# One planned order for all of attention, the channel MLPs and the second mixture's weights

## The chip, the cores and the metric

The kernel runs on one core of one Trainium2 chip. The metric is device time in microseconds (us) of one execution; lower is better. Engine names are those of the profile: PE (TensorE matmul), DVE (VectorE), ACT (ScalarE), POOL (GpSimd) and SP (SyncE, whose queue issues nearly all DMAs).

## What is computed

Four batches, 768 positions, 8 heads of 48, model width 384. First a linear attention with a complex decay per channel, then a mixture with a low-rank token mix and a channel MLP, then a second mixture with trigonometric gates:

```python
for t in range(S):                                  # attention, 768 steps
    S_re, S_im = ar * S_re - ai * S_im + kv, ar * S_im + ai * S_re
    y[:, :, t] = np.einsum('bhd,bhde->bhe', q[:, :, t], S_re)
...
h = xt @ U @ V                                      # first mixture
u = x + h.transpose(0, 2, 1)
x = u + np.maximum(u @ w_ch1, 0.0) @ w_ch2
...
theta = x @ w_theta                                 # second mixture
y = w_tok_r @ (x * cos(theta)) + w_tok_i @ (x * sin(theta))
u = x + y
out = u + np.maximum(u @ w_ch, 0.0)
```

The weights arrive as 64-bit floats and are unpacked on the chip into a high and a low 32-bit part, so most products are three matmuls (high by high, high by low, low by high).

## The kernel before, in words

**Attention.** The 768 positions are cut into 6 chunks of 128, and chunks go in pairs: 3 pairs for each batch, 12 in all. `ew` computes a pair's decay products on ACT and DVE in the store `er` (for pair 1 alone in the store made of `wa` and `wb`). For a pair this is some 20 operations over 128x768 elements, two kinds of scans (L358 and L385), and table loads on ACT. At its end four products a pair (L337, `tt2`) write what `gather` then moves by DMA into the tile `QK`. `pe_steps` then does a chunk on PE: scores (L453), their copy on ACT (L459) and mask on POOL (L463), transposes of k (L469), state update (L492), output (L521), a transpose back (L535), and `gx` (L546), which collects the low-rank product of a batch. When all six chunks of a batch are in, `g_steps` adds the low-rank mix to the batch's tokens (`hx`, L576 on PE, L581 on DVE). Only then can that batch's MLP start.

**MLP.** `mlp_steps` works on a batch as 3 groups of 256 tokens, and a group as 6 pairs of an F unit (18 matmuls, L711) and a C unit (12 matmuls, L736). So there are 72 of each. After an F unit, ACT writes `rh` (L716) and DVE `rl` (L721), which the next C unit reads. At a group's end DVE adds the result to the tokens (L741). The F units need the unpacked `w1` (9 jobs of `unpack`), the C units `w2` (12 jobs); a job is a DMA, one or two ACT operations and five on DVE (L610, L611, L613, L615, L311).

**Second mixture.** Its weights are unpacked by 16 jobs (4 for the wide weights, 12 for the token weights, six of which are written out to DRAM and read back later). Then `front` (L908, L920) makes the gates and `mix` (L971, L987) does the big products, up to the end.

**What sets the order.** Each engine runs its instructions in the order in which the program holds them. For batches 0 and 1 of attention, the unpacking of the first mixture's weights and the MLP of batch 0, a planner (`startup`) writes that order: every operation is a step with engines, a size, and the keys it reads and writes; `ranks` gives each step a number from the longest path behind it plus an entry of the table `LEAD`; `schedule` takes, among the steps that could start within 0.4 us of the earliest, the one with the lowest rank. `fixed` then emits the steps and ties each instruction to the one before it on the engines in `HELD`. Everything else (batches 2 and 3 of attention, the MLPs of batches 1 to 3, the second mixture) is emitted batch by batch in lanes, and a scheduler of the framework places it by lane priority; PE and SP are placed by it throughout:

```python
HELD = ('DVE', 'Activation', 'Pool')
```

Of the kernel before, what the change touches and what calls it, by code (L numbers as in the profile page):

```python
# [87 lines left out]
def schedule(steps, rank, bias, hop=HOP, window=400):  # L88
# [20 lines left out]
    while ready:  # L109
        cand, low = [], 1e18  # L110
        for n in ready:
# [77 lines left out]
def attn_moe_kernel(tc, pk, qn, kn, v, are, aim, U, V, w1, w2, wth, wtr, wti, wch, out):  # L189
# [98 lines left out]
    def load(pr, st):  # L288
# [4 lines left out]
        for z, name in enumerate(("re", ROWS[zi], "q", "kk")):  # L293
# [4 lines left out]
            ops.append(step(f, "D", 1300, [], [(st["key"], st["names"].get(name, name))]))  # L298
        return ops

    def load_v(g):
# [899 lines left out]
```

## Time and profile before

| | us |
|---|---|
| median of 3 timed runs (877.17 to 877.9) | 877.26 |
| the profiled execution: its time | 877.16 |
| its span, first to last instruction | 875.4 |
| PE busy in the span | 757.8 |
| DVE busy | 524.9 |
| ACT busy | 453.3 |
| POOL busy | 124.3 |

The span is what the profile shows, and 1.76 us of the execution lie around it. PE is busy for 87% of the span; PE's idle time, and the time in which its clock was granted at less than full speed, are what a new order can take away.

### The profile page before, as it was taken

How to read it: one execution, taken by the hardware profiler on the slowest of the kernel's cores; microseconds unless marked ns; L12 is line 12 of the kernel's file. 1: busy time of each engine (PE TensorE's matmuls, PEld its weight loads, DVE VectorE, ACT ScalarE, POOL GpSimd, SP SyncE). 2: the span in 40 equal slices, each digit the busy share in tenths (PEclk: the TensorE clock that was granted, in tenths of full speed). 3: DMA queues.
4: the chain of work that ended last, by engine and by line, in shares of the span. 5: the costliest groups of instructions: out<-in, count | busy, mean ns of one | idle time of the engine just before them, and what ended most of it. 6: DMA issues, size and time to landing. Idle time of an engine off the chain costs nothing.

```text
span 875.4 us, 13800 instructions
## 1 busy us (share of the span) xinstructions
PE 757.8 (87%) x5338; PEld 717.1 (82%) x5338; DVE 524.9 (60%) x787; ACT 453.3 (52%) x772; POOL 124.3 (14%) x144
## 2 busy tenths in 40 slices
PE   0085588798989698989999999899999999999996
PEld 0075367686978698979999999899999999999996
DVE  6958988978819578668151587893244335253321
ACT  6965876757726976784433253444155345253300
POOL 1011010200000002010101000000064234133200
PEclk9995867999998799999999999999999999999999
DMA  9264463552332443540331137620060000000001
GB/s 259 75 177 122 115 184 82 161 165 75 91 91 55 118 119 82 128 113 19 95 87 27 55 128 266 212 99 1 1 218 1 28 28 27 1 28 28 28 28 31
DMA packets 105657, 79.78 MB, mean 91 GB/s; under 512 B 32912, under 2 KB 97424, under 8 KB 105584
## 3 DMA queue, kind: packets, MB, share of 16 engines
q1 hardware_dynamic: 105184, 78.62, 32.2%
q8 instruction: 44, 0.72, 0.3%
q10 hardware_dynamic: 400, 0.20, 0.1%
q14 instruction: 29, 0.24, 0.1%
HBM read 50.33 MB, written 9.44 MB: 68 GB/s over the span
## 4 chain that ended last, share of the span: by engine, by line
PE 59%; DVE 15%; ACT 10%; DMA 8%; issue 3%; SPq 3%; POOL 0%; DVEq 0%; ACTq 0%; POOLq 0%
PE h L711 10%; PE c L736 9%; PE h L971 9%; PE c L971 9%; PE m L920 4%; PE m L987 4%; DVE er L337 4%; PE m L453 4%; PE m L521 4%; DMA er<-in_pk_dram 2%; ACT er L334 2%; DVE er L340 2%; PE m L492 2%; DMA tok1l<-tl 2%; ACT L334 2%
## 5 line engine op out<-in xcount | busy, mean ns | idle before, releaser
L711 PE MATMUL h<-uh,w1h 128*128 128x256 f32 x432 | 126.8, 294 | 3.1 <-DVE rl L721 2.1
L711 PE MATMUL h<-ul,w1h 128*128 128x256 f32 x432 | 125.0, 289 | 1.4 <-DVE ul L692 1.4
L711 PE MATMUL h<-uh,w1l 128*128 128x256 f32 x432 | 124.3, 288 | 0.0
L463 POOL TENSOR_SCALAR_AFFINE_SELECT pt<-pt 128x512 f32<-128x512 f32 x48 | 45.8, 962 | 425.7 <-ACT pt L459 411.2
L337 DVE TENSOR_TENSOR er<-er 128x768 f32<-128x768 f32 (+1 forms) x99 | 101.9, 1054 | 4.0 <-ACT er L334 2.0
L736 PE MATMUL c<-w2h,rl 128*128 128x384 f32 x288 | 100.1, 348 | 4.1 <-DVE rl L721 4.0
L736 PE MATMUL c<-w2h,rh 128*128 128x384 f32 x288 | 95.6, 349 | 6.7 <-ACT rh L716 3.0
L736 PE MATMUL c<-w2l,rh 128*128 128x384 f32 x288 | 97.8, 342 | 1.2 <-DVE w2l L311 1.1
L721 DVE SCALAR_TENSOR_TENSOR rl<-h,rh 128x512 fp32r<-128x512 f32 x72 | 49.3, 685 | 78.8 <-ACT rh L716 78.8
L711 PEld LDWEIGHTS h<-uh,w1h 128*128 128x128 f32 x432 | 83.5, 193 | 6.1 <-DVE rl L721 2.7
L711 PEld LDWEIGHTS h<-ul,w1h 128*128 128x128 f32 x432 | 83.6, 193 | 1.9 <-DVE ul L692 1.6
L711 PEld LDWEIGHTS h<-uh,w1l 128*128 128x128 f32 x432 | 83.5, 193 | 0.4 <-issue 0.2
L334 ACT ACTIVATE er<-er 128x768 f32<-128x768 f32 x88 | 74.0, 845 | 16.0 <-DVE er L337 12.4
L716 ACT ACTIVATE rh<-h 128x512 fp32r<-128x512 f32 x72 | 42.8, 596 | 67.4 <-PE h L711 59.5
L453 PE MATMUL m<-QK 96*128 96x128 f32 x384 | 60.0, 303 | 10.9 <-DMA QK<-wa 8.8
L453 PEld LDWEIGHTS m<-QK 96*128 96x128 f32 x384 | 53.5, 211 | 15.3 <-issue 10.5
L340 DVE SCALAR_TENSOR_TENSOR er<-er 128x768 f32<-128x768 f32 x55 | 52.8, 966 | 20.2 <-ACT er L334 11.6
L469 PE MATMUL m<-ident,QK 96*128 96x96 f32 x160 | 22.8, 261 | 46.0 <-DMA QK<-er 44.3
L736 PEld LDWEIGHTS c<-w2h,rh 128*128 128x128 f32 x288 | 52.8, 190 | 9.5 <-ACT rh L716 3.9
L736 PEld LDWEIGHTS c<-w2h,rl 128*128 128x128 f32 x288 | 54.6, 190 | 6.5 <-DVE rl L721 6.0
L469 PEld LDWEIGHTS m<-ident,QK 96*128 96x128 f32 x160 | 18.2, 150 | 49.6 <-issue 48.6
L736 PEld LDWEIGHTS c<-w2l,rh 128*128 128x128 f32 x288 | 54.3, 189 | 2.3 <-DVE w2l L311 1.8
(209 smaller groups left out, 1741.3 us busy)
## 6 DMA issues: line engine op xcount, KB each, us to landing
er<-in_pk_dram SPq DMA_DIRECT2D x88, 192.0 KB, 3.7
QK<-er SPq DMA_DIRECT2D x88, 145.1 KB, 3.4
x<-in_moe_w_ch_dram SPq DMA_DIRECT2D x9, 512.0 KB, 4.4
vt<-in_v_dram SPq DMA_DIRECT2D x48, 96.0 KB, 2.7
x<-in_moe_w_ch_dram SPq DMA_DIRECT2D x12, 384.0 KB, 3.4
st<-in_moe_w_tok_i_dram SPq DMA_DIRECT2D x6, 768.0 KB, 5.6
st<-in_moe_w_tok_r_dram SPq DMA_DIRECT2D x6, 768.0 KB, 4.2
out_dram<-x SPq DMA_DIRECT2D x23, 192.0 KB, 2.3
```

What stands on the lines that cost most here:

```text
L334: do("A", size, r, w, lambda e: A_.activation(out=out, in_=in_, func=func, **kw), tab)
L337: do("V", size, r, w, lambda e: V_.tensor_tensor(out=out, in0=in0, in1=in1, op=op))
L340: do("V", size, r, w, lambda e: V_.scalar_tensor_tensor(out=out, in0=in0, scalar=scalar, in1=in1, op0=op0, op1=op1))
L453: PE.matmul(ps[:, hh * T:(hh + 1) * T], lhsT=st["QK"][:, h, 1, 0:T], rhs=st["QK"][:, h, 0, 0:T], start=True, stop=True)
L463: G_.affine_select(out=pt, in_=pt, pattern=[[0, 4], [1, T]], compare_op=ALU.is_ge, fill=0.0, base=0, channel_multiplier=-1)
L469: PE.transpose(ps[:, hh * 96:(hh + 1) * 96], st["QK"][:, 4 * i + hh, 1, 0:T], ident[0:96, 0:96])
L521: PE.matmul(st["y"][64 * z:64 * z + 64, r * T:(r + 1) * T], lhsT=wide(old_w if k else vt_w, h), rhs=st["QK"][:, h, 0, 0:T] if k else st[f" ...
L711: PE.matmul(ps[:, f, :], lhsT=a[:, k, fs], rhs=u[:, k, :], start=(k == 0 and i == 0), stop=(k == NJ - 1 and i == 2))
L716: A_.activation(out=rh, in_=rts[n, p], func=AF.Relu)
L721: V_.scalar_tensor_tensor(out=rl, in0=ps, scalar=0.0, in1=r32(rh), op0=ALU.max, op1=ALU.subtract)
L736: PE.matmul(chs[n, t][:, 0:C], lhsT=r[:, f, t * T:(t + 1) * T], rhs=w[:, k, :], start=(k == 0 and i == 0), stop=(k == KF - 1 and i == 2))
L971: PE.matmul(ps[k][:, 0:C], lhsT=z[:, 2 * part + o, k * 128:(k + 1) * 128], rhs=w[:, s, ts], start=(s == 0 and part == 0 and j == 0), stop= ...
```

## The change

The planner now takes in all four batches of attention, all four MLPs, the check of the flags, the closing of the attention's buffers and the 16 unpacking jobs of the second mixture's weights, and it holds PE and SP to its order too. `attention` and `mains` are gone. What the planner knows is changed as well: the cost of some steps (the transfers' time to land is split into a part that holds the queue and a part after it, PE's unproven blocks cost 1.1 instead of 1.25 of their size), two keys `fo` and `co` that keep the F units and the C units each in their own order, one accumulator bank that is kept free, and one step that may run on DVE or ACT instead of ACT alone. The tiles `wa` and `wb` get the shape of five rows instead of one long one. `LEAD` holds a new number pair for every group of steps. The second mixture itself stays with the framework's scheduler.

```diff
 LEAD = {
-    'l0': (17.6, 55.3), 'e0': (1.2, 0.1), 'p0': (-49.1, -22.6), 'u': (-11.1, 38.3), 'x0': (283.2, 62.0),
...
+    'l0': (169.9, 1010.7), 'e0': (-3170.0, 1215.7), 'p0': (-720.0, -7.0), 'u': (2087.8, -1400.5),
...
-PLANNED = 2
+STAGED = 2
+
+PLANNED = 4
+
+LATER = {2: -60.0, 3: -60.0}
...
                 free = [x for x in frees[new[0][0]] if x is not None]
-                if not free:
+
+                if len(free) < 1 + (new[0][0] == "ps" and len(new[0]) > 2):
                     continue
...
-                    d = (1.05 if tab else 1.25) * size
+                    d = (1.05 if tab else 1.1) * size
...
-        at[e], end[n] = en, en + hop[e]
+        at[e], end[n] = en, en + (steps[n][5] if e == "D" and steps[n][5] else hop[e])
...
-        r0, dr = lead.get(nm, (0, 0))
+        r0, dr = lead.get(nm) or (LATER.get(batch_of(nm), 0), 0)
...
-    wa = wp.tile([128, KF * C], F32, tag="w", name="wa")
-    wb = wp.tile([128, KF * C], F32, tag="w", name="wb")
+    wa = wp.tile([128, 5, NR], F32, tag="w", name="wa")
+    wb = wp.tile([128, 5, NR], F32, tag="w", name="wb")
...
-        act(AF.Identity, n2, Bt, bias=b_magic, r=K("B"), w=K("n"), size=N + 100)
+        do(EL, (N + 100) / 2, K("B"), K("n"), lambda e: V_.tensor_scalar(
+            out=n2, in0=Bt, scalar1=MAGIC, scalar2=None, op0=ALU.add) if e == "V" else
+            A_.activation(out=n2, in_=Bt, func=AF.Identity, bias=b_magic))
...
-            do("P", 18 * 119, [("u", n % 2)] + [("w1", p // 2, k) for k in range(NJ)], [m], mm)
+            do("P", 18 * 119, [("u", (b * NB + n) % 2)] + [("w1", p // 2, k) for k in range(NJ)], [m, "fo"], mm)
...
-                do("P", 6 * 174, [kr, ("w2", 2 * p), ("w2", 2 * p + 1)], [m], lambda e, t=t: mm(e, t))
+                do("P", 6 * 174, [kr, ("w2", 2 * p), ("w2", 2 * p + 1)], [m, "co"], lambda e, t=t: mm(e, t))
...
-    HELD = ('DVE', 'Activation', 'Pool')
+    HELD = ('DVE', 'Activation', 'Pool', 'PE', 'SP')
...
-        ops = mlp_steps(0)
-        steps.extend(ops)
-        names.extend("m0" if o[1] == "P" else "mv" for o in ops)
+        for b in range(PLANNED):
+            ops = mlp_steps(b)
+            steps.extend(ops)
+            names.extend(MAIN[b] if o[1] == "P" else f"mv{b or ''}" for o in ops)
+
+        used = sorted({k for o in steps for k in (*o[3], *o[4])
+                       if k[0] in ("E", "W", "gps", "pcf") or str(k)[:2] in ("qk", "pt", "kn", "vt", "a0", "a1", "ca", "u4", "v4", "gp")},
+                      key=str)
+        job("open", [step(flags, "V", 1000, [], used), step(flag_sum, "P", 0, [], used), step(reopen, "V", 6, [], used + ["p2"])])
+        for n, ops in enumerate(mix2_jobs()):
+            job(f"t{n}", ops)
         rank = ranks(steps, names, LEAD)
         done = schedule(steps, rank, BIAS)
```

What this does to the instructions is seen at three places. Lines are those of each kernel; in the changed one L337 is L374, L340 is L377, L610 to L615 are L649 to L654, L721 is L760, L453 is L492, L469 is L508, L521 is L560, L492 is L531 and L711 is L750.

The first is DVE at the four products that end pair 1 (store `wa` and `wb`), with what each row waits for. Before:

```order
L337 TENSOR_TENSOR wb<-wa,wb 128x3x2x128 [waits Activation_49]
L337 TENSOR_TENSOR wa<-wa,wb 128x3x2x128 [waits DVE_49,Activation_49]
L337 TENSOR_TENSOR wb<-wa,wb 128x3x2x128 [waits DMAHW5_49,DMAHW6_49,DMAHW1_49,DMAHW7_49,DMAHW0_49,DVE_49]
L337 TENSOR_TENSOR wa<-wa,wb 128x3x2x128 [waits DVE_49]
L311 TENSOR_TENSOR w1l<-x,w1h 128x512 [waits Activation_49]
```

And after the change:

```order
L374 TENSOR_TENSOR wb<-wa,wb 128x3x2x128 [waits Activation_49]
L649 TENSOR_SCALAR x<-x 128x192
L650 TENSOR_SCALAR x<-x 128x192 [waits DVE_49]
L374 TENSOR_TENSOR wa<-wa,wb 128x3x2x128 [waits Activation_49]
L374 TENSOR_TENSOR wb<-wa,wb 128x3x2x128
L374 TENSOR_TENSOR wa<-wa,wb 128x3x2x128 [waits DVE_49]
```

The third product no longer waits for DMAs; two rows of an unpacking job stand between the first two.

The second is DVE some four rows after the last add of batch 0's low-rank mix, where the MLP of batch 0 begins (`er` is the next pair's store, `x` the staging area of the weight jobs, `rl` the low part after an F unit). Before:

```order
L721 SCALAR_TENSOR_TENSOR rl<-h,rh 128x512
L613 SCALAR_TENSOR_TENSOR x<-x 128x384
L615 SCALAR_TENSOR_TENSOR x<-x 128x384
L340 SCALAR_TENSOR_TENSOR er<-er 128x6x128
L311 TENSOR_TENSOR w2l<-x,w2h 128x384
L358 SCALAR_TENSOR_TENSOR er<-er,d_101 128x774
L340 SCALAR_TENSOR_TENSOR er<-er 128x6x128
L610 TENSOR_SCALAR x<-x 128x384
L611 TENSOR_SCALAR x<-x 128x384
L613 SCALAR_TENSOR_TENSOR x<-x 128x384
L615 SCALAR_TENSOR_TENSOR x<-x 128x384
L501 TENSOR_TENSOR a_st_111<-m,QK 96x4x2x48
```

And after the change:

```order
L760 SCALAR_TENSOR_TENSOR rl<-h,rh 128x512
L649 TENSOR_SCALAR x<-x 128x384
L650 TENSOR_SCALAR x<-x 128x384
L652 SCALAR_TENSOR_TENSOR x<-x 128x384
L760 SCALAR_TENSOR_TENSOR rl<-h,rh 128x512
L654 SCALAR_TENSOR_TENSOR x<-x 128x384 x2
L348 TENSOR_TENSOR w2l<-x,w2h 128x384 x2
L374 TENSOR_TENSOR er<-er 128x12x128
L760 SCALAR_TENSOR_TENSOR rl<-h,rh 128x512
L422 SCALAR_TENSOR_TENSOR er<-ones,er 128x257 x2
L649 TENSOR_SCALAR x<-x 128x384
L650 TENSOR_SCALAR x<-x 128x384
```

Rows of `rl` and of the weight jobs have come forward, and rows of the pair have gone back.

The third is PE at one chunk of attention, from its scores to its first output rows. Before, at chunk 8 (counted from 0), the rows begin so:

```order
L453 MATMUL m_1275<-QK_1188 128x128 x4
L453 MATMUL m_1286<-QK_1188 128x128 x4
L469 MATMUL m_1296<-ident_78,QK_1188 128x96 x4
L711 MATMUL h_1389<-uh_888,w1h_128 128x256
L711 MATMUL h_1389<-uh_888,w1l_129 128x256
L711 MATMUL h_1389<-ul_889,w1h_128 128x256
L711 MATMUL h_1389<-uh_888,w1h_128 128x256
L711 MATMUL h_1389<-uh_888,w1l_129 128x256
L711 MATMUL h_1389<-ul_889,w1h_128 128x256
L711 MATMUL h_1389<-uh_888,w1h_128 128x256
L711 MATMUL h_1389<-uh_888,w1l_129 128x256
L711 MATMUL h_1389<-ul_889,w1h_128 128x256
```

Nine more of these matmuls and four transposes follow before the chunk's first output row (L521). After the change, at chunk 22:

```order
L492 MATMUL m_4007<-QK_3932 128x128 x4
L492 MATMUL m_4012<-QK_3932 128x128 x4
L508 MATMUL m_4025<-ident_78,QK_3932 128x96 x4
L508 MATMUL m_4032<-ident_78,QK_3932 128x96 x4
L560 MATMUL m_4040<-pt0_4017,vt0_106 64x128 x2
L560 MATMUL m_4040<-QK_3932,a_st1_112 64x128 x2
L560 MATMUL m_4040<-pt0_4017,vt0_106 64x128 x2
L560 MATMUL m_4040<-QK_3932,a_st1_112 64x128 x2
L531 MATMUL m_4050<-vt0_106,kn_4037 96x96 x8
```

Here only eight transposes stand between the scores and the first output row.

## Rows read from the trace of the kernel before

**Rows 1.** Windows by stage: busy us of each engine, granted clock, DMA share, GB/s.

```profile
0.00:142.00 142.00, 66.25 (x445) 53.77 (x445) 114.41 (x162) 103.74 (x159) 15.27 (x36) 0.82 0.58 148
142.00:500.00 358.00, 328.86 (x2631) 305.13 (x2632) 231.59 (x331) 208.33 (x351) 33.92 (x36) 0.96 0.36 94
142.00:200.00 58.00, 52.66 (x432) 48.51 (x434) 48.37 (x77) 35.95 (x66) 7.93 (x8) 0.92 0.55 150
500.00:639.00 139.00, 133.97 (x928) 130.74 (x928) 87.97 (x134) 52.72 (x84) 2.02 (x2) 1.00 0.35 118
639.00:862.00 223.00, 223.00 (x1307) 222.08 (x1306) 88.31 (x156) 88.04 (x180) 73.07 (x70) 1.00 0.11 37
```

**Rows 2.** Waits of PE, 0 to 142 us: total us, times, longest.

```profile
PE m L469 <- DMA QK<-er: 44.3, 1, 44.3
...
PE m L521 <- POOL pt L463: 6.7, 4, 2.2
```

**Rows 3.** Waits of DVE, 0 to 142 us, the longest.

```profile
DVE wb L337 <- DMA QK<-wb: 9.5, 1, 9.5
```

**Rows 4.** Timeline of DVE around that wait: start, busy, idle before.

```profile
57.30 0.96 DVE L337 TENSOR_TENSOR wa<-wa,wb 128x768 f32<-128x768 f32 x1
67.72 0.96 DVE L337 TENSOR_TENSOR wb<-wa,wb 128x768 f32<-128x768 f32 x1 [9.46 <-DMA QK<-wb]
```

**Rows 5.** Groups of DVE by shape: count, busy us, mean ns, idle before.

```profile
L721 DVE SCALAR_TENSOR_TENSOR rl<-h,rh 128x512 fp32r<-128x512 f32 x72 | 49.3, 685 | 78.8 <-ACT rh L716 78.8
...
L613 DVE SCALAR_TENSOR_TENSOR x<-x 128x384 uint32<-128x384 uint32 x12 | 7.3, 609 | 0.4
...
L615 DVE SCALAR_TENSOR_TENSOR x<-x 128x384 uint32<-128x384 uint32 x12 | 6.7, 558 | 0.4
L311 DVE TENSOR_TENSOR w2l<-x,w2h 128x384 fp32r<-128x384 f32 x12 | 6.7, 555 | 3.1 <-ACT w2h L622 3.0
...
L610 DVE TENSOR_SCALAR x<-x 128x384 f32<-128x384 f32 x12 | 5.2, 434 | 1.1 <-ACT x L609 1.1
...
L611 DVE TENSOR_SCALAR x<-x 128x384 uint32<-128x384 uint32 x12 | 4.3, 357 | 0.3
```

**Rows 6.** An F unit and a C unit in the chain that ended last: start, us.

```profile
611.16 2.13 PE h L711 x18
613.29 2.11 PE c L736 x12
```

**Rows 7.** Timeline of PE: the six parts of a chunk of attention, at full clock.

```profile
421.51 1.79 PE m L453 x16
...
463.02 0.82 PE L469 MATMUL m<-ident,QK 96*128 96x96 f32 x8
...
467.07 1.36 PE m L492 x16
468.42 1.91 PE m L521 x32
...
447.62 0.60 PE L535 MATMUL m<-ident,yT 128*128 128x128 f32 x4
...
450.99 0.81 PE L546 MATMUL gps<-x,u 128*96 128x384 f32 x2
```

**Rows 8.** Waits of PE, 142 to 500 us.

```profile
PE m L492 <- ACT kn L422: 8.5, 2, 6.9
...
PE c L736 <- ACT rh L716: 2.4, 2, 1.4
PE up L682 <- DVE rl L721: 2.1, 1, 2.1
PE h L711 <- DVE rl L721: 2.1, 2, 1.8
```

**Rows 9.** Timeline of PE: matmuls of the first F unit, start to start.

```profile
142.55 0.41 PE L711 MATMUL h<-ul,w1h 128*128 128x256 f32 x1
142.76 0.41 PE L711 MATMUL h<-uh,w1h 128*128 128x256 f32 x1
```

**Rows 10.** Group of ACT, 500 to 639 us: what its unpacking rows waited for.

```profile
L609 ACT ACTIVATE tl<-st 128x768 f32<-128x768 f32 (+1 forms) x16 | 13.9, 867 | 25.4 <-DMA tok1l<-tl 11.0 <-DMA st<-in_moe_w_tok_r_dram 9.1 <-DMA st<-in_moe_w_theta_dram 2.3
```

More of the change, by code (lines that the diff above doesn't have):

```diff
@@ L158, in schedule, with batch_of @@
     return sorted(out)
+MAIN = [f"m{b}" for b in range(PLANNED)]
+def batch_of(name):
+    per = {"l": NQ, "e": NQ, "p": NC, "x": NC, "g": 1}.get(name[0])
+    return int(name[1:]) // per if per and name[1:].isdigit() else 0
 def ranks(steps, names, lead, hop=HOP):
@@ L277, in attn_moe_kernel, with stages @@
         G_.memset(st["rows"][8][:, :, 0:1], 0.0)
+    def stages(b, c):
+        i = ((b - STAGED) * NC + c) * C
+        return sorted({("s0", "h0", "h1")[j // 1536] for j in (i, i + C - 1)}) if b >= STAGED else []
     EL = 'AV'
@@ L359, in ew @@
             out=flat(4), data0=flat(8), data1=d1.rearrange("p j c t -> p (j c t)"), initial=0.0, op0=ALU.mult, op1=ALU.add))
-        do("A", 6, K("A"), [("pc", pr)], lambda e: A_.copy(out=pcf[:, pr], in_=rows[4][:, :, T]))
+        do("A", 6, K("A"), [("pcf", pr)], lambda e: A_.copy(out=pcf[:, pr], in_=rows[4][:, :, T]))
         act(AF.Abs_reciprocal_sqrt, Dt, P2, "R", r=K("A"), w=K("D"))
@@ L779, in run, with flags @@
             f(engs[0])
-    def attention(b):
-        gps = {}
-        for pr in range(b * NQ, (b + 1) * NQ):
-            run(load(pr, e_store))
-            run(ew(pr, e_store))
-            for g in (2 * pr, 2 * pr + 1):
-                a, m = pe_steps(g, gps)
-                run(a + m)
-        run(g_steps(b, gps))
+    env = {}
+    def flags(e):
+        fr = const.tile([128, 4], F32, name="fr")
+        V_.tensor_reduce(out=fr[:, 0:1], in_=flg, axis=mybir.AxisListType.X, op=ALU.max)
+        V_.tensor_reduce(out=fr[:, 1:2], in_=pcf.rearrange("p g j c -> p (g j c)"), axis=mybir.AxisListType.X, op=ALU.min)
+        V_.tensor_scalar(out=fr[:, 0:1], in0=fr[:, 0:1], scalar1=0.0, scalar2=None, op0=ALU.is_gt)
+        V_.tensor_scalar(out=fr[:, 1:2], in0=fr[:, 1:2], scalar1=P2_MIN, scalar2=None, op0=ALU.is_le)
+        V_.tensor_tensor(out=fr[:, 2:3], in0=fr[:, 0:1], in1=fr[:, 1:2], op=ALU.max)
+        V_.memset(fr[:, 3:4], 1.0)
+        env["fr"] = fr
@@ new lines, in flag_sum, with reopen @@
+    def flag_sum(e):
+        psf = ps_m.tile([128, 512], F32, tag="m", name="m")
+        fr = env["fr"]
+        PE.matmul(psf[0:1, 0:1], lhsT=fr[:, 2:3], rhs=fr[:, 3:4], start=True, stop=True)
+        env["psf"] = psf
+    def reopen(e):
+        V_.tensor_copy(out=fl_i, in_=env["psf"][0:1, 0:1])
+        at.close()
+        p2 = ctx.enter_context(tc.tile_pool(name="p2", bufs=1, reuse_waits="tile"))
+        dr = ctx.enter_context(tc.tile_pool(name="dr", bufs=1, space=bass.MemoryType.DRAM))
+        jb = ExitStack()
+        env.update(jb=jb, jp=jb.enter_context(tc.tile_pool(name="jb", bufs=2, reuse_waits="tile")),
+                   tok=[p2.tile([128, NC, S], F32R, name=f"tok0{y}") for y in "hl"],
+                   tokd=[dr.tile([128, NC, S], F32, name=f"tok1{y}") for y in "hl"],
+                   **{n: p2.tile([128, NJ, C], F32R, name=n) for n in ("wthh", "wthl", "wchh", "wchl")})
@@ new lines, in later, with wrap, f, mix2_jobs @@
+    def later(n, make):
+        cell = []
+        def wrap(j):
+            def f(e):
+                if not cell:
+                    cell.extend(make(True))
+                cell[j][0](e)
+            return f
+        return [(wrap(j), *o[1:]) for j, o in enumerate(make(False))]
+    def mix2_jobs():
+        jobs = []
+        def some(real, tag):
+            return env["jp"].tile([128, 1536 if tag == "st" else S], F32 if tag == "st" else F32R, tag=tag, name=tag) \
+                if real else stg[0]
+        def wide_job(nm, src, sc, k0, nk, key):
+            def make(real):
+                hi, lo = [env[nm + y][:, k0:k0 + nk, :] if real else xs[0][:, 0:nk, :] for y in "hl"]
+                sl, tl = some(real, "st"), some(real, "tl")
+                return unpack(hi, lo, src[k0 * 128:(k0 + nk) * 128, :].rearrange("(k p) d -> p k d", p=128), nk * C,
+                              sl, [key], r=["p2"], scale=sc, shape="p (k d) -> p k d", tf=r32(tl)[:, 0:nk * C])
+            return make
+        def tok_job(x, src, i, key):
+            def make(real):
+                sl = some(real, "st")
+                if x:
+                    hi, lo = [some(real, "t" + y)[:, 0:S] for y in "hl"]
+                    tf = None
+                else:
+                    hi, lo = [t[:, i, :] for t in env["tok"]] if real else [stg[0][:, 0:S]] * 2
+                    tf = r32(some(real, "tl")[:, 0:S])
+                ops = unpack(hi, lo, src[i * 128:(i + 1) * 128, :], S, sl, [key], r=["p2"], tf=tf)
+                def put(e):
+                    for y, a in enumerate((hi, lo)):
+                        nc.sync.dma_start(out=env["tokd"][y][:, i, :], in_=r32(a))
+                if x:
+                    ops.append(step(put, "D", 1300, [key], [key], 2400))
+                return ops
+            return make
+        todo = [wide_job(nm, src, sc, k0, nk, f"j{k0 // 2}") for nm, src, sc in (("wth", wth, INV2PI), ("wch", wch, None))
+                for k0, nk in ((0, 2), (2, 1))]
+        todo += [tok_job(x, src, i, f"j{i % 2}") for x, src in ((1, wti), (0, wtr)) for i in range(NC)]
+        return [later(n, make) for n, make in enumerate(todo)]
@@ L797, in job @@
             names.extend([name] * len(ops))
-        for b in range(PLANNED):
+        for b in range(B):
             gps = {}
```

89 lines of the change are left out of this document (19 added, 70 removed), and 42 rows, old and new, of the table LEAD.

## The prediction

> **What bounds the kernel now.** I read the windows by stage first. The span of 875.4 us has four stages, and each has another limit [rows 1]. From 0 to 142 us, where the first F unit starts, PE is busy for only 66.25 us: its longest wait, 44.3 us, is for the first `QK` [rows 2]. DVE is busy 114.41 of the 142, so this stage is as long as DVE's work up to batch 0's low-rank mix, plus DVE's own holes. From 142 to 500 us, up to the end of attention, PE is busy 328.86 of 358, so 29.1 us idle, at a granted clock of 0.96, which costs another 0.04 x 358 = 14.3. Together 43.4 us are lost there, and 314.6 are PE's work. DVE has 231.59 us in it: no bound for the stage as a whole, but in its first part, 142 to 200, it is busy 48.37 of 58, a share of 0.83. From 500 to 639 us (the rest of the MLPs, beside the unpacking of the second mixture's weights) PE loses 5.0. From 639 to 862 us PE is never idle and the clock is full. After that the output drains. What an order can win therefore lies before 639 us: 43.4 and 5.0 on PE, and DVE's holes ahead of 142.
>
> **The first stage.** DVE's largest hole is a single one of 9.46 us [rows 3, 4]: the third of pair 1's four products waits until the transfers out of `wb` have landed. The order of the changed kernel shows that product without a wait for a DMA (first place above); the tiles' new shape lets the two halves be told apart. DVE is what the stage waits for, so I count the hole as won. What comes due next is pair 2's own chain, for which the order has unpacking rows as filler. Against it, the new order puts a whole `w1` job ahead of pair 0's first sum on DVE. A `w2` job costs 0.434 + 0.357 + 0.609 + 0.558 + 0.555 = 2.51 us [rows 5], and a `w1` job is a third wider: 3.3. Since the DVE work up to batch 0's last add is the same (I added the rows of either order at their groups' mean times: 118.8 us before, 117.2 now), a job moved ahead costs only if pair 0's chain starts later and DVE then stands. I charge all of it: **9.5 - 3.3 = 6.2 us won**, with 0 and 9.5 as bounds.
>
> **The second stage.** The new order has the same count of attention rows ahead of the first F unit (all six chunks of batch 0), but goes on differently. Up to the first add of an MLP result, DVE's rows sum to 72.1 us before and 37.6 now: before, most of pair 3's products and scans stand among them, now they hold seven weight jobs and seven `rl` rows at 0.685 (second place above). On PE, nine F units and six and a half C units now stand in one run before the next scores. At 2.13 and 2.11 us [rows 6] that is 19.2 + 13.7 = 32.9 us.
>
> What PE loses now I take from DVE's work against PE's, stretch by stretch, as in each of them the longer one counts. DVE's share is between 0.83, the row of 142 to 200, and 114.41 / (142 - 9.5) = 0.86, the first stage without its hole.
> First group: 37.6 / 0.83 = 45.3 (or 43.7 at 0.86) against 32.9: 12.4 (10.8) lost.
> From there to batch 1's last low-rank add: DVE has 118.6 - 37.6 = 81.0 us, so 97.6 (94.2); PE has nine F units, ten and a half C units, and six chunks at 1.79 + 0.82 + 1.36 + 1.91 + 0.60 + 0.81 = 7.3 us [rows 7], with some 2.5 for the small transposes and mixes: 19.2 + 22.2 + 43.8 + 2.5 = 87.7. Lost: 9.9 (6.5).
> From there to the end of attention: DVE has 137.6 us (166 at 0.83), PE 23 F units, 22 C units and twelve chunks, 49.0 + 46.4 + 87.6 = 183. PE bounds, and nothing is lost to DVE.
> What an in-order PE loses besides is short covers. Between a chunk's first scores and its first output row, ACT must copy and POOL must mask. With chunks counted from 0, in chunks 6 to 23 the old order holds 3.8 us of PE work or more between them, 7.7 in the mean; the new one 6.4 in the mean, but under 2.1 at four of them (third place above). In batch 0, where before has such short covers, PE waited for that mask 4 times, 6.7 us in all [rows 2]. Four more such waits: 6.7.
> Sum of losses: 29.0 (24.0). I take 26, near the middle, so **17.4 us won** from the 43.4. Bounds: 43.4 (nothing won) and 5 (DVE without a hole, 37.6 - 32.9, and covers that hold).
>
> When attention ends, the new order has done 738 of the 1,296 F matmuls and 468 of the 864 C matmuls, the old one 765 and 492. That is 1.5 F units and 2 C units, 7.4 us of PE work, moved from the second stage into the third: nothing in sum, as PE is the bound of both.
>
> **The third stage.** Its 5.0 us come from ACT and DVE rows of the unpacking that stand waiting for transfers (25.4 us of ACT's waiting [rows 10]) with `rh` and `rl` behind them. In the new order these rows are planned with the transfers' time. I take 2.0 left, **3.0 won**, between 0 and 5.0. The cover is ample: 16 jobs, PE work of some 140 us.
>
> **The second mixture.** The same instructions. Fewer of batch 0's gate projections (L920) stand ahead of the last C unit: 9 matmuls now, 27 before. They are only moved, but the gates' chain on ACT and DVE starts later by as much. I allow **1.0 lost**, between 0 and a C unit, 2.11.
>
> **The sum**, against the profiled execution's own span: 875.4 - 6.2 - 17.4 - 3.0 + 1.0 = 849.8 us; with the 1.76 us outside the span 851.6. That execution took 877.16, the median of the timed runs is 877.26, so no correction: **852 us**.
>
> **A rule that speaks against it.** In the old trace the first F unit's matmuls start 0.21 us apart [rows 9] and those of a warm unit 2.13 / 18 = 0.118: the first stage's clock is 0.82 in the mean, with PE idle more than half of it. The Trainium skill, "TensorE: Matmul & The Clock Gate", section "HAM oscillation — how this bites in real kernels", says that a matmul loop with gaps in it falls back to half clock after each gap and pays the warm-up each time. By that rule the first group, where PE waits for weight jobs between units, would run at half clock throughout. The trace agrees for the first stage; the stretch 142 to 200 us, with 5.3 us idle, had 0.92.
>
> **Rivals.**
> (a) *Half clock in the first group.* Each unit waits for two weight jobs, PE's clock stays at 1.2 GHz, and 32.9 us become 32.9 x 0.21 / 0.118 = 58.6, more than DVE's 44.5. That is 14 us on top: 866. For it: the first stage's clock. Against it: PE has 74% to do there, and 142 to 200 shows 0.92.
> (b) *Only the hole.* The losses of the second stage are of the pairs' chain (ACT and DVE in turns, one 6.9 us wait for `kn` [rows 8]), and a new order moves them about but keeps 43.4: 852 + 17.4 = 869. For it: DVE is busy only 65% in that stage, so its waits are not for lack of rows.
> (c) *More than forecast.* DVE at nearly full share with good filler, loss 10 instead of 26, hole won whole: 852 - 16 - 3 = 833.
> (d) *Slower: PE stands behind its own order.* The planner's times set PE's order now. Where a chunk's chain (scores, copy, mask; transposes, `kn`) comes later than planned, all matmuls behind it wait, F units too, and with 0.83 of DVE taken every copy may be late. The Trainium skill, "PSUM — Partial Sum Buffer", section "Engine vs sequencer instructions", says that matmuls start and complete in program order; the trace agrees, as PE ran nothing in its 6.9 us for `kn`. Priced at the longest mask wait seen, 2.2 us [rows 2], for each of 18 chunks: 852 - 6.7 + 39.6 = 885. It decides from (877.2 - 845.3) / 18 = 1.8 us a chunk. Against it: covers are 6.4 us in the mean, three times that.
>
> **Chances.** Forecast (842 to 862) 0.46, (c) 0.18, (a) and (b) together (862 to 875) 0.20, within 0.2% of before 0.05, (d) 0.11. A measurement of this kernel tells about 0.2%, 1.75 us, from no change. Faster is the forecast, (a), (b) and (c): 0.84. The range must leave out no more than 0.2: 834 to 876 drops (d) and half of (c). The forecast's own range is 842 to 862.
>
> **What would show it.** DVE's 9.46 us hole gone and the first F unit near 136 us, else the first step is wrong. PE's first 33 us of MLP stretched to 42 to 46 us with waits for `w2l` or `rl`, and a clock above 0.85, else (a). From 136 us to the last low-rank add some 334 us, PE's loss near 26, else (b) or (c). Waits of L560 for POOL or of L531 for `kn` of some 7 us; above 32 us in all would be (d). The third stage with under 3 us of PE idle, and PE without a hole from the last C unit on. The prediction falls if batch 1's attention, whose DVE work is set back by 21 us (97.5 to 118.6), lets PE run dry before its low-rank adds.

## The result, and the profile after

The changed kernel takes 839.69 us (median of four runs, 839.3 to 843.75), the kernel before 877.58 on the same chip: a ratio of 0.9576 with a 95% interval of 0.9545 to 0.9608. That is faster, and 12.3 us below the forecast of 852: inside its range of 834 to 876, but below the forecast's own narrower range of 842 to 862. The profiled execution spans 838.4 us and took 840.06.

Windows of both kernels by the same four milestones follow: start, first F unit, last low-rank add, last C matmul, end. Columns are those of [rows 1]. First the kernel before, whose first stage is 141.96 us long:

```profile
141.96:495.77 353.81, 324.67 (x2601) 300.94 (x2602) 229.86 (x328) 207.53 (x349) 33.92 (x36) 0.96 0.35 92
495.77:640.66 144.89, 139.86 (x967) 136.63 (x966) 90.76 (x141) 55.22 (x89) 2.67 (x3) 1.00 0.37 126
640.66:875.40 234.74, 227.06 (x1330) 225.82 (x1328) 89.89 (x159) 86.89 (x178) 72.42 (x70) 0.99 0.11 35
```

Then the changed kernel:

```profile
0.00:133.99 133.99, 60.57 (x447) 50.53 (x447) 114.82 (x168) 100.37 (x157) 15.62 (x36) 0.84 0.62 162
133.99:457.95 323.96, 310.42 (x2556) 287.67 (x2556) 241.38 (x335) 199.28 (x334) 35.42 (x36) 0.99 0.39 101
457.95:599.57 141.62, 140.42 (x987) 139.15 (x986) 90.30 (x134) 50.02 (x77) 0.00 (x0) 1.00 0.34 122
599.57:838.40 238.83, 231.10 (x1353) 229.40 (x1352) 91.92 (x166) 92.17 (x189) 74.40 (x72) 1.00 0.11 34
```

The stages changed by -8.0, -29.9, -3.3 and +4.1 us, -37.0 together. "Lost" is again PE's idle time plus what the clock's shortfall costs (length times one minus the granted clock). In the second stage it was 29.1 + 0.04 x 354 = 43.3 us and is 13.5 + 0.01 x 324 = 16.8; the clock is printed to two digits, so each of these is good to 2 us. So 26.5 of the 29.9 us are loss that went away, and 3.4 are work that moved. The counts of PE's matmuls show what only moved: 45 have left the second stage (2601 to 2556), 20 more stand in the third (net) and 23 more in the last, whose PE busy time grows by 4.0 us (227.06 to 231.10).

The hole on DVE [rows 3, 4] is gone. In DVE's timeline (start, duration, line, tiles, count, idle time before) pair 1's four products stand together, with two rows of a weight job between the first two:

```profile
69.20 0.95 DVE L374 TENSOR_TENSOR wb<-wa,wb 128x768 f32<-128x768 f32 x1
70.07 0.25 DVE L649 TENSOR_SCALAR x<-x 128x192 f32<-128x192 f32 x1
70.36 0.26 DVE L650 TENSOR_SCALAR x<-x 128x192 uint32<-128x192 uint32 x1
70.69 0.96 DVE L374 TENSOR_TENSOR wa<-wa,wb 128x768 f32<-128x768 f32 x1
71.56 0.95 DVE L374 TENSOR_TENSOR wb<-wa,wb 128x768 f32<-128x768 f32 x1
72.55 0.96 DVE L374 TENSOR_TENSOR wa<-wa,wb 128x768 f32<-128x768 f32 x1
```

The first group of MLP units, up to the first add of a result (L780), then up to batch 1's low-rank adds, then the rest of the second stage, in windows:

```profile
133.99:166.72 32.73, 32.73 (x233) 32.73 (x233) 31.26 (x58) 19.49 (x32) 0.00 (x0) 0.96 0.29 89
166.72:260.30 93.58, 87.36 (x737) 79.66 (x737) 77.89 (x97) 68.33 (x115) 11.60 (x12) 1.00 0.45 114
260.30:457.95 197.65, 190.33 (x1589) 175.28 (x1589) 132.22 (x184) 111.46 (x187) 23.82 (x24) 0.99 0.38 96
```

PE is never idle in the first group, at a clock of 0.96, and DVE is busy 31.26 of 32.73 us, a share of 0.955. The three stretches lose 1.3, 6.2 and 9.3 us, which make up the 16.8. What PE waits for in the whole second stage (line, releaser, us in total, times, longest), to be held against [rows 8]:

```profile
PE m L508 <- DMA QK<-er: 3.2, 7, 1.4
PE m L574 <- ACT yT L570: 1.9, 1, 1.9
PE gps L585 <- ACT kn L461: 1.3, 1, 1.3
PE c L775 <- DVE rl L760: 1.2, 1, 1.2
PE m L560 <- POOL pt L502: 1.1, 4, 0.3
...
PE h L750 <- DVE ul L731: 0.4, 1, 0.4
```

The longest wait for `kn`, 6.9 us before, is 1.3 now, and waits for the mask (POOL) come to 1.1 us.

### The profile page after: what moved, and what is told of

The parts are those of the page before. It is cut to its first block, busy times and chain, and to the rows that moved or that the text cites. A ratio compares the mean times of both kernels' runs of the same rounds, so it can differ in the third digit from the quotient of the medians.

```text
span 838.4 us, 13782 instructions
## 1 busy us (share of the span) xinstructions
PE 742.5 (89%) x5338; PEld 706.8 (84%) x5338; DVE 538.4 (64%) x801; ACT 441.9 (53%) x756; POOL 125.4 (15%) x144
## 4 chain that ended last, share of the span: by engine, by line
PE 58%; DVE 14%; DMA 8%; ACT 7%; SPq 6%; issue 5%; POOL 1%; DVEq 0%; ACTq 0%; POOLq 0%
PE h L750 10%; PE c L775 9%; PE h L1036 9%; PE c L1036 9%; PE m L1052 4%; PE m L985 4%; DVE er L374 4%; PE m L560 3%; PE m L492 3%; DMA QK<-er 3%; SPq L444 2%; PE m L531 2%; ACT er L371 2%; DMA st<-in_moe_w_tok_i_dram 2%; DMA x<-in_moe_w_ch_dram 2%
## 5 line engine op out<-in xcount | busy, mean ns | idle before, releaser
L750 PE MATMUL h<-uh,w1h 128*128 128x256 f32 x432 | 124.9, 289 | 1.4 <-DVE rl L760 0.9
L750 PE MATMUL h<-uh,w1l 128*128 128x256 f32 x432 | 122.1, 283 | 0.0
L750 PE MATMUL h<-ul,w1h 128*128 128x256 f32 x432 | 122.1, 283 | 0.0
L374 DVE TENSOR_TENSOR er<-er 128x768 f32<-128x768 f32 (+1 forms) x99 | 104.6, 1076 | 9.6 <-ACT er L371 4.5
L502 POOL TENSOR_SCALAR_AFFINE_SELECT pt<-pt 128x512 f32<-128x512 f32 x48 | 47.7, 1001 | 390.1 <-ACT pt L498 378.6
L775 PE MATMUL c<-w2h,rh 128*128 128x384 f32 x288 | 102.5, 356 | 0.1
L775 PE MATMUL c<-w2h,rl 128*128 128x384 f32 x288 | 97.5, 339 | 1.2 <-DVE rl L760 1.2
L750 PEld LDWEIGHTS h<-uh,w1h 128*128 128x128 f32 x432 | 81.8, 189 | 3.6 <-DVE rl L760 1.6
L750 PEld LDWEIGHTS h<-uh,w1l 128*128 128x128 f32 x432 | 81.9, 190 | 0.5
L750 PEld LDWEIGHTS h<-ul,w1h 128*128 128x128 f32 x432 | 81.9, 190 | 0.0
L760 DVE SCALAR_TENSOR_TENSOR rl<-h,rh 128x512 fp32r<-128x512 f32 x72 | 49.4, 688 | 49.1 <-ACT rh L755 48.6
L492 PE MATMUL m<-QK 96*128 96x128 f32 x384 | 57.2, 302 | 13.7 <-DMA QK<-wa 11.0
L377 DVE SCALAR_TENSOR_TENSOR er<-er 128x768 f32<-128x768 f32 x55 | 53.5, 975 | 24.2 <-ACT er L371 17.5
L492 PEld LDWEIGHTS m<-QK 96*128 96x128 f32 x384 | 52.5, 212 | 18.0 <-issue 14.7
L508 PE MATMUL m<-ident,QK 96*128 96x96 f32 x160 | 22.5, 270 | 48.6 <-DMA QK<-er 48.1
L508 PEld LDWEIGHTS m<-ident,QK 96*128 96x128 f32 x160 | 17.9, 153 | 51.8 <-issue 45.7
```

The costliest lines, as they stand in the source:

```text
L374: do("V", size, r, w, lambda e: V_.tensor_tensor(out=out, in0=in0, in1=in1, op=op))
L377: do("V", size, r, w, lambda e: V_.scalar_tensor_tensor(out=out, in0=in0, scalar=scalar, in1=in1, op0=op0, op1=op1))
L492: PE.matmul(ps[:, hh * T:(hh + 1) * T], lhsT=st["QK"][:, h, 1, 0:T], rhs=st["QK"][:, h, 0, 0:T], start=True, stop=True)
L502: G_.affine_select(out=pt, in_=pt, pattern=[[0, 4], [1, T]], compare_op=ALU.is_ge, fill=0.0, base=0, channel_multiplier=-1)
L508: PE.transpose(ps[:, hh * 96:(hh + 1) * 96], st["QK"][:, 4 * i + hh, 1, 0:T], ident[0:96, 0:96])
L750: PE.matmul(ps[:, f, :], lhsT=a[:, k, fs], rhs=u[:, k, :], start=(k == 0 and i == 0), stop=(k == NJ - 1 and i == 2))
```

## The experiments

My theory after this result was that the new order of DVE's and ACT's rows (weight jobs and `rl` ahead of the pairs' products) makes the gain, and that PE follows it. The rival was that holding PE itself to the plan makes it. The table gives all runs; stage figures are of each one's profiled execution, which can lie up to 7 us off its median (e11). The kernel before had medians of 875.8 to 876.8 us beside them; the changed kernel was not timed beside them, so it is compared with them by the ratios. The intervals of e2, e5, e8, e9 and e11 overlap that of the changed kernel: differences of 1 to 4 us between them are not clear of noise.

| kernel | us | ratio to before (95%) | first F unit | 2nd stage, us (lost) | 3rd | after last C |
|---|---|---|---|---|---|---|
| before | 877.58 | 1 | 141.96 | 353.8 (43.3) | 144.9 | 234.7 |
| changed | 839.69 | 0.9576 (0.9545-0.9608) | 133.99 | 324.0 (16.8) | 141.6 | 238.8 |
| e1 old order, new shape | 873.33 | 0.9964 (0.9944-0.9984) | 134.29 | 355.5 (45.1) | 145.2 | 234.4 |
| e2 new order, old shape | 843.28 | 0.9618 (0.9588-0.9648) | 138.35 | 327.2 (18.8) | 140.0 | 238.9 |
| e3 new order, PE, SP free | 881.44 | 1.0066 (1.0033-1.0099) | 132.82 | 363.8 (53.3) | 138.7 | 239.4 |
| e4 old order, PE, SP held | 864.42 | 0.9862 (0.9832-0.9893) | 135.53 | 344.6 (33.1) | 147.0 | 234.5 |
| e5 new order, SP free | 842.06 | 0.9616 (0.9585-0.9646) | 133.94 | 325.2 (18.4) | 142.3 | 239.2 |
| e6 new order, PE free | 881.6 | 1.0061 (1.0024-1.0098) | 136.92 | 366.7 (56.4) | 138.0 | 239.2 |
| e7 new scope, no table | 906.69 | 1.0346 (1.0317-1.0375) | 124.77 | 369.4 (65.3) | 163.0 | 246.3 |
| e8 first group, DVE longer | 842.57 | 0.9621 (0.9595-0.9647) | 134.36 | 327.6 (19.6) | 140.0 | 238.5 |
| e9 n2 on ACT | 842.2 | 0.9615 (0.9585-0.9645) | 136.04 | 327.3 (19.1) | 140.5 | 239.1 |
| e10 mask twice | 871.79 | 0.9951 (0.9927-0.9976) | 143.90 | 342.9 (35.9) | 141.8 | 239.4 |
| e11 weights' low parts on POOL | 840.56 | 0.9602 (0.9575-0.9630) | 138.00 | 327.3 (18.5) | 142.1 | 238.7 |
| e12 no table, PE, SP free | 924.64 | 1.0565 (1.0534-1.0595) | 129.58 | 384.6 (79.3) | 159.5 | 244.8 |

**e1 and e2: the tiles' shape by itself.** e1 adds it to the kernel before, e2 takes it out of the changed one:

```diff
-    wa = wp.tile([128, KF * C], F32, tag="w", name="wa")
+    wa = wp.tile([128, 5, NR], F32, tag="w", name="wa")
```

(and `wb` alike; the line that takes rows out of them is changed to match).

> The kernel before with one part of the change alone: wa and wb allocated in the shape in which they are used; its table, its scope and its held engines stay. My theory (DVE sets the first stage, and the 9.46 us hole is a wait for the whole tile): the hole goes, the first F unit starts 8 to 9.5 us earlier, and as the rest of that order is untouched the program ends as much earlier, 868 to 869.5 us. Rival (the hole hides another wait of nearly its length): first F unit within 2 us of 142, time 875 to 877.

> The changed kernel with that one part undone: wa and wb in the old long shape, every engine's order the same. My theory: the hole comes back at pair 1's third product, the first F unit starts 8 to 9.5 us later, and since PE is busy for 95% and more of what follows, all of it reaches the end: 847.5 to 849.5 us. Rival (the new order has slack behind the first stage, so that a late start is caught up in the first group of MLP units): 840 to 843 us.

In e1 the first F unit starts 7.7 us earlier, nearly as expected, but the program gains only 3.2 us by its ratio (1.4 to 4.9) and 6.1 by its profile: part of the early start is lost again, 1.7 us of it in the second stage of that profile. In e2 the first F unit is 4.4 us later and the median 3.6 higher, which fits, though the intervals of the two ratios overlap. In DVE's waits of e2's first stage the wait is back, but short:

```profile
DVE wb L374 <- DMA QK<-wb: 3.5, 1, 3.5
```

In e4, where PE and SP are held as well and the shape is the old one, it is 4.2 us. So the 9.5 us [rows 3] were not the price of the shape in any order; in these two kernels, with PE and SP held, the wait is about 4.

**e3 to e6: who is held.** One line is changed. For e3:

```diff
-    HELD = ('DVE', 'Activation', 'Pool', 'PE', 'SP')
+    HELD = ('DVE', 'Activation', 'Pool')
```

e4 is the reverse of it in the kernel before, e5 leaves out `'SP'` alone, e6 `'PE'` alone.

> The changed kernel with PE and SP out of the list of engines that are held to the plan; DVE, ACT and POOL keep the plan's order in attention and MLPs. My theory (the gain is in the order of DVE's and ACT's rows: weight jobs and rl ahead of the pairs' products, which PE follows): within 4 us of the changed kernel, 836 to 844 us, and perhaps 1 to 2 us better after the last C unit, where more gate projections may stand ahead of it. Rival (holding PE is what gives the gain of the second stage): the loss of 42 us comes back there, 855 us or more.

> The kernel before with that other part alone: PE and SP held to the old plan as well, where it reaches (two batches of attention, one of MLPs). My theory: the old plan has DVE's pair rows ahead of the weight jobs still, so the second stage's loss stays at 40 us or so; 870 to 882 us. Rival (holding PE is the gain): 850 to 860 us.

My theory falls: by the traces, e3 has exactly the changed kernel's order on DVE, ACT and POOL up to the end of attention, and it gains nothing; its second stage loses 53 us, more than before. e4 wins 12 us with the old plan.

> The changed kernel with SP alone out of the list of held engines; the rows of PE, DVE, ACT and POOL stand exactly as in the changed kernel, only the DMA issues on SP's queue are in another order. After the run with both free came to 881 us, my theory is: it is PE's order that makes the gain of the second stage, SP's adds some 5 us in the first stage (where the wait for wb was 9.5 us with SP free and 3.5 to 4.2 with SP held). 838 to 848 us. Rival (SP's queue brings pairs and weights in time, PE's order follows): 865 to 885 us.

> The changed kernel with PE alone out of the list of held engines; SP, DVE, ACT and POOL keep the plan. My theory (PE's order is the cause): 870 to 885 us, with 30 us and more of PE idle between the first F unit and the last low-rank add. Rival (SP's order is the cause): 838 to 850 us.

This settles which of the two it is: PE. With SP free the time stays within 2.4 us, with PE free all is lost. The 5 us that I gave to SP's order in the first stage did not show: the first F unit of e5 starts at 133.94. The window of e6's second stage:

```profile
136.92:503.62 366.70, 332.26 (x2582) 303.93 (x2581) 241.20 (x335) 198.10 (x333) 31.74 (x36) 0.94 0.34 87
```

DVE's busy time is that of the changed kernel (241.20 and 241.38), PE is idle for 34 us and its clock is 0.94. Where the two part is seen by stretches:

| stretch of the second stage, us | changed | e6 |
|---|---|---|
| first group of MLP units | 32.7 | 33.7 |
| to the end of batch 1's low-rank adds | 95.0 | 109.9 |
| to the last low-rank add | 196.3 | 223.1 |

So the new order of DVE and ACT is enough for the short first group, and PE's order decides the rest. PE's largest waits in e6's second stage:

```profile
PE c L775 <- ACT rh L755: 8.6, 4, 2.9
PE m L560 <- POOL pt L502: 4.4, 2, 4.1
PE c L775 <- DVE x L780: 2.9, 1, 2.9
```

One of those waits for `rh`, first on PE, then in ACT's timeline beside it:

```profile
360.31 0.60 PE L574 MATMUL m<-ident,yT 128*128 128x128 f32 x4
361.48 0.89 PE L585 MATMUL gps<-x,u 128*96 128x384 f32 x2 [0.57 <-ACT x L461]
365.10 0.62 PE L775 MATMUL c<-w2h,rh 128*128 128x384 f32 x2 [2.74 <-ACT rh L755]
```

```profile
359.01 0.56 ACT L570 COPY yT<-m 128x512 f32<-128x512 f32 x1
359.48 0.22 ACT L408 ACTIVATE er<-er 128x6 f32<-128x6 f32 x1
360.95 0.48 ACT L461 COPY x<-m 128x384 f32<-128x384 f32 x1 [1.26 <-PE m L574]
361.32 0.85 ACT L371 ACTIVATE er<-er 128x768 f32<-128x768 f32 x1
362.19 1.28 ACT L414 ACT_TABLE_LOAD   x1
363.49 0.20 ACT L414 ACTIVATE cb<-er 128x1 f32<-128x1 f32 x1
363.72 0.84 ACT L415 ACTIVATE er<-er 128x768 f32<-128x768 f32 x1
364.47 0.58 ACT L755 ACTIVATE rh<-h 128x512 fp32r<-128x512 f32 x1
```

PE wants the next C unit at 362.4. The `rh` that it needs stands in ACT's order behind the copy of `x`, three rows of the pair's chain and a table load of 1.28 us, and that copy had itself waited 1.26 us for PE's transposes (L574). ACT is held to one order, PE runs another, and each waits for the other in turn. The order of the changed kernel has, at this chunk, 18 F matmuls between those transposes and L585 and only then the C unit; the free order has nothing between L574, L585 and the C unit. Earlier in the same chunk, from its first scores (L492) to its last output rows (L560), the free order runs 78 attention matmuls in one lump; the held one puts 6 C matmuls and 18 F matmuls between rows of the same kinds and counts. Over the whole second stage, by the traces, the held order has F matmuls in 37 runs and attention in 59, the free one 66 and 72. This is one wait of many. PE's waits for ACT add up to some 17 us of the 34 in e6 and 3.4 in the changed kernel; that all of them arise in this way is not shown.

**e7 and e12: the table.** `LEAD = {}` in the changed kernel, e12 with PE and SP free besides.

> The changed kernel with an empty table: the planner, the scope and the five held engines stay, and the ranks are those of the longest path through the steps alone. My theory (a joint order that PE is held to is worth something, but which order it is matters as much): between the old order with PE and SP held and the changed kernel, 848 to 862 us. Rival 1 (scope and holding do it all): 838 to 843. Rival 2 (all is in the table): 875 us or more.

> The changed kernel with an empty table and with PE and SP free: the fourth corner beside the changed kernel (table, held: 840), the one with the table and free engines (881) and the one with no table and held engines (907). Theory 1 (holding PE is worth what the order is worth to which it is held, and the order without a table is a poor one): freeing PE and SP moves it by less than 10 us, 897 to 915. Theory 2 (holding is worth 12 us or more with any order, as it was with the old one): 919 us or more. Theory 3 (holding PE to a poor order costs more than it gives): under 895.

I had expected e7 between the two kernels; it is 30 us slower than before. So the wider scope and the hold together do not make up for a poor order: that e7's first F unit starts earliest of all, at 124.77, does not help it. e12 bears out theory 2: holding PE and SP is worth 12 us with the old plan, 18 without a table (924.64 - 906.69) and 42 with the new table (881.44 - 839.69). The gain needs both, the order and PE held to it. No run has the new table with the old scope or with the old costs and keys, so what they add to the table stays open.

**e8: how full DVE can be.** One row of a `w2` job is done twice in the seven jobs of the first group:

```diff
...
+        return o[:5] + [step(lambda e: (o[5][0](e), o[5][0](e)), *o[5][1:])] + o[6:] if i in (4, 6, 7, 8, 9, 10, 11) else o
```

> The changed kernel with one row of some 0.56 us done twice on DVE in each of the seven w2 jobs of the first group of MLP units (the result is the same), 3.9 us more of DVE's work there, the order the same. It measures how full DVE can be there. In the changed kernel that group takes 34 us with DVE busy 32.5. If DVE can be filled to 0.95, the group becomes (32.5 + 3.9) / 0.955 = 38.1 us, 4 us longer; if 0.86 were its limit, as the forecast had it, (32.5 + 3.9) / 0.86 = 42.3, 8 us longer; if DVE is not what the group waits for, less than 1 us longer. The whole program gets at most as much longer: 840 to 844 by the first.

```profile
134.36:171.68 37.32, 35.06 (x234) 33.80 (x234) 34.97 (x65) 19.53 (x32) 0.00 (x0) 0.94 0.26 78
```

The group, here counted from the first F unit (the expectation starts it 1.3 us earlier), grows by 4.6 us for 3.7 us of rows, at a share of 34.97 / 37.32 = 0.94. So this group gets longer when DVE has more to do in it, and 0.86 is not DVE's limit.

**e9: `n2`.** Nine rows go back to ACT, at their places:

```diff
-        do(EL, (N + 100) / 2, K("B"), K("n"), lambda e: V_.tensor_scalar(
-            out=n2, in0=Bt, scalar1=MAGIC, scalar2=None, op0=ALU.add) if e == "V" else
+        do(EL, (N + 100) / 2, K("B"), K("n"), lambda e:
             A_.activation(out=n2, in_=Bt, func=AF.Identity, bias=b_magic))
```

> The changed kernel with its nine n2 rows (0.56 us each on DVE) done on ACT instead, at the same places of the order; this undoes the part of the change that lets n2 run on either engine. Theory (PE's order, which is the same, holds enough cover): ACT's rows cost it some 0.85 us each, DVE is 5.0 us freer, and the program moves by less than 2 us: 838.5 to 842. Rival (taking these rows off ACT was needed, since the masks and rh wait for ACT): 845 us or more.

842.2 us lies 0.2 above the first expectation, and its interval overlaps that of the changed kernel: no effect is shown, and this part of the change explains little of the gain.

**e10: late masks.**

```diff
-            do("G", 330, [f"pt{i}"], [f"pt{i}"], lambda e, i=i: select(e, i))
+            do("G", 330, [f"pt{i}"], [f"pt{i}"], lambda e, i=i: (select(e, i), select(e, i)))
```

> The changed kernel with POOL's mask done twice in each half of each of the 24 chunks (the result is the same), so that every chunk's masked scores come some 0.65 to 1.3 us later; all orders are kept. It measures what a late input costs a PE that is held to its order. Theory (the planned covers are long, thin at four chunks, and batch 0 has PE idle anyway): 2 to 6 us, 842 to 846. Rival (a held PE has no slack, every late input is lost, as the slower case of the forecast had it): 24 x 0.65 to 24 x 1.3, 855 to 871 us.

The rival was right, and its range, up to 871, was even 0.8 short. PE's waits for the mask, on the first line in the second stage, on the last in the first:

```profile
PE m L560 <- POOL pt L502: 17.4, 14, 3.1
...
PE m L560 <- POOL pt L502: 14.0, 5, 5.5
```

They were 1.1 and 4.3 us in the changed kernel. POOL is busy 34.6 us more in the second stage (70.03 instead of 35.42), 0.96 us for each of the 36 masks there. That makes the second stage 19.0 us longer, 1.05 us for each of its 18 chunks, and the first 9.9 us, 1.65 for each of six. Not all of that need be the masks' lateness: with the same 335 rows in the second stage, DVE is busy 5.8 us longer beside the busier POOL (247.16 instead of 241.38).

**e11: a try at a faster version.** The low parts of the first MLP's weights go to POOL:

```diff
-        do("V", n, lambda e: tt(e, out=lo, in0=tv, in1=r32(hi), op=ALU.subtract), w)
+        do("V", n, lambda e: tt("G" if w and w[0][0] in ("w1", "w2") else e, out=lo, in0=tv, in1=r32(hi), op=ALU.subtract), w)
```

> The changed kernel with the low parts of the first MLP's weights (21 subtractions, w1l and w2l) done on POOL instead of DVE, at the same places of the order. Up to the first F unit that takes nine rows of 0.685 and five of 0.55 us off DVE, 8.9 us, and some 3.8 more in the first group. Theory (the first stage is as long as DVE's work): the first F unit 4 to 9 us earlier, 831 to 836 us, faster than both kernels. Rival (the pairs' chain from ACT to DVE sets that stage, or POOL's rows, over 1 us each, keep the weight buffers and the masks longer): 838 us or more.

No gain: 840.56 us is what the rival said. The profiled execution lies 7.3 us above the median, so its stage lengths say little by themselves. DVE has 14 rows fewer in the first stage, 8.9 us of work, but its busy time falls only from 114.82 to 112.43. Two stretches of its profile, DVE first and then POOL:

```profile
48.48 0.96 DVE L377 SCALAR_TENSOR_TENSOR wb<-wb 128x768 f32<-128x768 f32 x1
49.54 1.77 DVE L395 TENSOR_TENSOR_SCAN wa<-wb,d 128x774 f32<-128x774 f32 x1
...
61.52 1.92 DVE L377 SCALAR_TENSOR_TENSOR wb<-wb 128x768 f32<-128x768 f32 x1
63.47 1.27 DVE L374 TENSOR_TENSOR wb<-wb,wa 128x768 f32<-128x768 f32 x1
```

```profile
49.74 2.63 POOL L348 TENSOR_TENSOR w1l<-x,w1h 128x512 fp32r<-128x512 f32 x1 [5.44 <-ACT w1h L661]
...
61.35 1.27 POOL L348 TENSOR_TENSOR w1l<-x,w1h 128x512 fp32r<-128x512 f32 x1 [7.80 <-ACT w1h L661]
62.65 2.58 POOL L502 TENSOR_SCALAR_AFFINE_SELECT pt<-pt 128x512 f32<-128x512 f32 x2
```

The row at 61.52 takes 1.92 us beside POOL's subtraction, the same form at 48.48 takes 0.96; and POOL's subtraction at 49.74, begun during DVE's scan, takes 2.63, the one at 61.35 takes 1.27. So part of what DVE is rid of comes back as longer rows, and the masks stand behind POOL's new rows: PE waits 6.9 us for them in the first stage of this profile, 4.3 in that of the changed kernel. None of the runs beats the changed kernel.

## Why the prediction was right or wrong

Direction and place were right: the gain lies before the last C unit, most of it in the second stage, and rival (b), that a new order moves the losses about but keeps them, fell. Sizes were off in both directions, so part of the forecast's nearness is luck: too much loss was put into the first group and the waits for masks, none into the stretch after batch 1's low-rank adds. And the step that most of the gain hangs on, PE's hold, stood nowhere in the sum.

**The first stage, 6.2 us forecast, 8.0 measured.** Bounds 0 and 9.5 hold. The hole went as said. The 3.3 us charged for the `w1` job were too much: pair 0's first sum on DVE starts at 12.39 instead of 10.80 us, 1.6 later. What I read wrongly is the hole's owner. With PE and SP held and the old shape it is 3.5 to 4.2 us (e2, e4), so of the 8.0 us the shape brings 4.4 in the new order (by one profile of each, e2), and the rest comes with the order itself.

**The second stage, a loss of 26 forecast, 16.8 measured.** This is the step that was mis-sized, in three of its four terms.

"First group: 12.4 (10.8) lost" measured 1.3, all of it the clock: the group took 32.7 us instead of 43.7 to 45.3. Two things were wrong in it. DVE's share is 0.955, not 0.83 to 0.86. And 37.6 us is a sum of row times (36.4 in the new trace), while the share is one of occupied time: rows overlap at their ends, and 2.9 us of them run ahead of the first F unit, so DVE is busy for only 31.26 us in the group. At 0.83 these would have taken 37.7 us; the share thus explains 4.9 of the 12.6 us from 45.3 to 32.7, and the sum 7.6. What the old share of 0.83 was made of, DVE's waits from 142 to 200 us show:

```profile
DVE rl L721 <- ACT rh L716: 5.1, 3, 3.2
DVE w2l L311 <- ACT w2h L622: 2.3, 4, 1.4
```

In the new first group the largest such line is:

```profile
DVE rl L760 <- ACT rh L755: 0.4, 2, 0.2
```

So the share was not low because of the pairs' rows (0.2 us of waits): the same kinds of rows that fill the new group had to wait for ACT there, and find their inputs ready here. e8 agrees with 0.94.

"Four more such waits: 6.7" measured 1.1 for all mask waits of the stage: batch 0's price of up to 2.2 us a wait was not theirs. The middle term, 9.9 (6.5) up to batch 1's low-rank adds, came to 93.58 - 87.36 = 6.2 us, and batch 1's later pairs did not let PE run dry. The size is right, and so is DVE's share there (77.89 of 93.58, 0.83), but only 1.4 of the 6.2 us are waits for a row of DVE; the largest are 1.9 for `yT` and 1.3 for `kn`, both of ACT, so the reason given is not shown. For the rest of the stage, where "nothing is lost", PE lost 9.3: 7.3 idle, 3.0 of it for the pairs' transfers (`QK`), and 2.0 to the clock. Neither was in the sum.

**What the sum left out.** I took PE's planned order as given and asked only what DVE and the covers cost in it. That it is the hold on PE which brings the gain stood nowhere in the forecast but in rival (d), as a danger. The runs show that the gain hangs on it: the same order on DVE, ACT and POOL gives 881 us with PE free (e3, e6) and 840 with PE held. By itself it is not enough, since without the table a held PE gives 907 (e7). The old loss of 43.4 us was then not DVE's lack of rows alone; three engines were held to a plan and PE ran another order. How much of the 43.4 that is can't be split off exactly: with the old plan, holding PE and SP takes 10 us of it (e4).

**Rival (d) itself** did not happen, but its price was real. It was to decide from 1.8 us a chunk; e10 makes each of a chunk's two masks 0.96 us longer and loses 1.05 us a chunk in the second stage, 1.65 in the first, 29 in both, and ends 0.5% under before. My argument against it, a cover of 6.4 us in the mean, does not hold: PE waited for the mask 14 times in the second stage's 18 chunks, in spite of that mean. The new order is good for the latencies as they are, with little in reserve.

**The third stage, 3.0 forecast.** PE's idle time there fell from 5.0 to 1.2 us, 3.8 won, and it did so with PE free as well (1.4 in e3, 1.3 in e6), but not in e1 and e4, which have the old unpacking (5.2 and 4.7). So this gain comes with the new plan and not with PE's hold. That planning the unpacking rows with their transfers is enough for it is not borne out: e7 and e12 plan them too, without the table, and PE is idle there for 15.0 and 18.2 us, mostly waiting for `rl`.

**The second mixture, 1.0 lost forecast, 4.1 longer.** PE's idle time there is 7.7 us as before; the stage is longer by PE's work (4.0 us more), with 23 more matmuls, 18 of them gate projections that no longer stand ahead of the last C unit. The third stage is rid of them. That belongs to the new order and not to PE's hold, since e3 and e6 have it too. I priced it as a loss; it is a transfer.

With the 7.4 us of moved work, the second stage was forecast to become 24.8 us shorter, the third and last together 5.4 longer. They became 29.9 shorter and 0.8 longer; with the first stage's 1.8 that is the 11.4 us from 849.8 to the span of 838.4. Rival (a) did not come about: the first group ran at a granted clock of 0.96 of 2.4 GHz, with no gap in it that could have tested it. Over the second stage the clock fell with PE's idle time: 0.99 with 13.5 us idle, 0.94 in e6 with 34.4, 0.92 in e12 with 48.5. Rival (c), whose 833 is nearer to the time than the forecast, had the share right for the first group alone and the hole too large.

## What to carry to other kernels

Where some engines are held to a plan, hold the one that feeds on them too: with DVE and ACT in the new order and PE in another, all of the gain was gone. The order must be a good one, though: held to the one without the table, the kernel was 30 us slower than before. A share of busy time read in one order says little of another: look at what the waits in it were for, and whether the same rows wait in the new order. Don't divide a sum of row times by a share of occupied time, as rows overlap. Test an order that works by making one short input later everywhere: here 1 us on each mask cost some 30 us, so such an order wants to be made anew when any latency in it changes.

## What the runs showed of the hardware

DVE and POOL delay each other's rows: in e11 a DVE row of 0.96 us took 1.92 beside a POOL row. The mask takes 0.63 us at best, 1.0 in the mean and 2.2 at most in the changed kernel, which fits, though it is not shown that DVE's rows make all of that difference. The Trainium skill, "SBUF — State Buffer", section "Summary: rules for kernel authors", says that a DVE instruction with two inputs in SBUF and a POOL instruction that reads SBUF exclude each other, and that the later one waits for the whole of the other. The trace agrees to 0.25 us in the rows shown: at 61.52, 1.10 us of POOL's row were left and DVE's became 0.96 longer; at 49.74, 1.57 us of the scan were left and POOL's row became 1.36 longer than the one at 61.35. I had not counted this when I moved rows to POOL.
